# The last batch's second expert, run on 32 places in column tiles amid the main products

## The chip, the cores and the metric

One NeuronCore of a Trainium2 chip runs the whole program. The metric is the time of one execution on the device in microseconds; lower is better. Of each kernel there are several timed runs and one profiled execution, in which every instruction and DMA transfer is recorded. Engines: PE (TensorE, matrix products), DVE (VectorE), ACT (ScalarE), POOL (GpSimd), SP (SyncE, which here only issues DMA). Each engine takes its instructions strictly in order and waits on semaphores.

## The reference

Attention with 16 query heads and one key/value head, then a two-level mixture of experts on the result: a group is chosen per row, then an expert in the group.

```
scores = scale * q @ k^T ; attn = softmax(scores) ; out = attn @ v     # 8 batches, 16 heads, 384 rows, 64 wide
x = out, heads joined                                                  # 3072 rows x 1024
g_idx = argmax(x @ w_group)        ; g_w = softmax weight of the choice
e_idx = argmax(x @ w_expert[g])    ; e_w = softmax weight of the choice
y[row] = g_w * e_w * (relu(x[row] @ w1[g, e]) @ w2[g, e])              # 16 experts, 1024 x 1024 each
```

All inputs are random draws; rows of one batch are so alike that each of the batches 0 to 6 chooses one expert for all its 384 rows. Batch 7 chooses one expert for 363 rows and a second for 21.

## The kernel before, in words

**Order.** The order on every engine is written out by hand (`tc.manual_schedule`). A loop over 96 slots (line 794) does the attention: scores, softmax, transposes and the products with v, and, amid them, the expert of the batch before. An expert is a Python generator (`expert`, line 472) that yields after every four products and after each reading-out; `advance(n)` (line 710) takes 3n steps of it, so one `advance(1)` is one group of eight products with what reads it. An expert has eight groups of the first layer (L479, 128 x 384 in bfloat16, relu into `h_t`) and six of the second (L493, 128 x 512): three blocks j of 128 rows by two halves nh of the columns.

**Rows.** `main_expert` runs the most frequent expert of a batch on all 384 rows, each scaled by its gate weight (`gsel`), which is zero for a row that chose another. Each block of rows is stored by four DMAs of SP (L536, 32 rows of 4 KB each).

**The second expert of batch 7** has code of its own, `few_*`. `few_turn` turns xb back into rows (L587). `few_flags` and `few_places` give each row of the second expert a place by a running sum over the rows. With at most 128 such rows the expert is dealt with here, else it is left for the loop at the end. `few_places` makes a 0/1 matrix `sel` of 128 places per block. `few_gather` (L643) brings the rows to their places by products with `sel`, and (L654) the gate weight and the row's number in several bfloat16 parts. `few_expert` computes the hidden layer (L674: 64 products, 128 places) and the result (L689: 24 products), scales it (L693, L695), and one indirect DMA of POOL (L696) writes it over the 128 rows, places without a row being out of bounds. That DMA waits until the main stores have landed.

**The tail** (lines 827 to 908) is after slot 96: rest of batch 6's expert, last attention products, `load_second(0)` and `load_second(1)` (w1 and w2 of the second expert: POOL's DMAs with a cast from float32 to bfloat16, two halves each, L454; two buffers for w1 and two for w2, so the second expert's w2 waits for batch 6's last L493), then batch 7's main expert with the `few_*` steps between its groups, the gate arithmetic for the loop, `keep_xb` (L470, the last batch's xb to DRAM for the loop, 768 KB), `few_expert`. The loop at the end (L911) makes one pass for each (batch, expert) still open; here none.

**PSUM.** `xbank()` hands out four banks in turn (pool `ps_x`), `bank_end()` the four banks of the score tiles (`ps_s`, name `sb`) once attention has ended.

Of the kernel before, what the change touches and what calls it, by code (L numbers as in the profile page):

```python
# [19 lines left out]
def kernel(  # L20
# [24 lines left out]
    NR = 4096  # L45
    assert NR > N
# [9 lines left out]
    w2f = moe_w2.rearrange("g e (fo fi) d -> (g e) fi fo d", fi=P)  # L56

# [393 lines left out]
    def load_w(e, n):  # L451
        w = wpool.tile([P, KO, F], BF16, tag=f"w{n + 1}", name="w")
        for o in range(0, KO, 4):
            nc.gpsimd.dma_start(  # L454
                out=w[:, o:o + 4, :], in_=(w1f, w2f)[n][ds(e, 1), :, o:o + 4, :].rearrange("o p c f -> (o p) c f")
            )
        return w
# [72 lines left out]

    def main_expert(b, on_act):
        w1, w2 = st.pop(("w", b))

        def store(j, y):
            for n in range(QN):
                nc.sync.dma_start(out=out_v[b, j, n], in_=y[32 * n:32 * (n + 1), :])  # L536

        yield from expert(st["xb", b], w1, w2, scaled(lambda: st["gsel", b][0], store), any_bank, on_act)

    def few_ready():  # L540
# [4 lines left out]
        for name, t, widths in (  # L545
            ("16", c16, (("eye", P), ("tri", P), ("sel", ST * P), ("f", 4), ("cum", 4), ("parts", 5 * ST))),
            ("32", c32, (
                ("cols", P), ("tri", P), ("sel", ST * P), ("prod", ST * GE), ("ohs", GE), ("rows", ST), ("rest", ST), ("row", 1), ("pos", 4),
                ("f", ST), ("fits", 1), ("gate", 1), ("low", 1), ("at", 1),
# [7 lines left out]
            fw["cols32"], pattern=[[1, P]], base=0, channel_multiplier=0, allow_small_or_imprecise_dtypes=True  # L557
# [9 lines left out]

        rows, parts = fw["rows32"], fw["parts16"].rearrange("p (j t) -> p j t", t=5)
        nc.gpsimd.iota(
            rows, pattern=[[P, ST]], base=(B - 1) * S - NR, channel_multiplier=QN, allow_small_or_imprecise_dtypes=True  # L570
        )
        for n in range(QN):
            nc.gpsimd.memset(fw["low32"][32 * n:32 * (n + 1), :], float(n * (1 - 32 * QN)))
        nc.gpsimd.tensor_tensor(
            out=rows, in0=rows, in1=fw["low32"].to_broadcast([P, ST]), op=ALU.add
        )
        nc.gpsimd.tensor_copy(out=parts[:, :, 3], in_=rows)
        nc.gpsimd.tensor_tensor(out=parts[:, :, 4], in0=rows, in1=parts[:, :, 3], op=ALU.subtract)
        fw["xt"] = [ppool.tile([P, Dm], BF16, tag="pr", name="xtok") for _ in range(ST)]
        fw["xg"] = ppool.tile([P, KO, P], BF16, tag="pr", name="xg")  # L580
# [28 lines left out]
    def few_places():  # L609
# [6 lines left out]
        nc.vector.tensor_single_scalar(out=fw["fits32"], in_=pos[:, 3:4], scalar=float(P), op=ALU.is_le)  # L616
# [4 lines left out]
        for j in range(ST):  # L621
            nc.vector.tensor_scalar(
                out=fw["sel32"][:, ts(j, P)], in0=fw["cols32"], scalar1=pos[:, j:j + 1], scalar2=fw["f32"][:, j:j + 1],
                op0=ALU.is_equal, op1=ALU.mult,
            )
        nc.scalar.copy(out=fw["sel16"], in_=fw["sel32"])

    def few_parts():
        fw, gsel = st["few"], st["gsel", B - 1][1][:]
        parts, rest = fw["parts16"].rearrange("p (j t) -> p j t", t=5), fw["rest32"]  # L630
        nc.gpsimd.tensor_copy(out=parts[:, :, 0], in_=gsel)
        nc.gpsimd.tensor_tensor(out=rest, in0=gsel, in1=parts[:, :, 0], op=ALU.subtract)
        nc.gpsimd.tensor_copy(out=parts[:, :, 1], in_=rest)
        nc.gpsimd.tensor_tensor(out=parts[:, :, 2], in0=rest, in1=parts[:, :, 1], op=ALU.subtract)

    def few_gather():
        fw = st["few"]
        parts = fw["parts16"].rearrange("p (j t) -> p j t", t=5)
        for half in range(2):
            bank = xbank()  # L640
            for k in range(4):
                for j in range(ST):
                    nc.tensor.matmul(  # L643
                        out=bank[:, ts(k, P)], lhsT=fw["xt"][j][:, ts(4 * half + k, P)], rhs=fw["sel16"][:, ts(j, P)],
                        start=(j == 0), stop=(j == ST - 1),
                    )
            xg = fw["xg"][:, 4 * half:4 * half + 4, :].rearrange("p k t -> p (k t)")
            if half:
                nc.vector.tensor_copy(out=xg, in_=bank[:])
            else:  # L650
                nc.scalar.copy(out=xg, in_=bank[:])
        bank = xbank()
        for j in range(ST):
            nc.tensor.matmul(  # L654
                out=bank[:, 0:5], lhsT=fw["sel16"][:, ts(j, P)], rhs=parts[:, j, :], start=(j == 0), stop=(j == ST - 1)
            )
        nc.vector.tensor_reduce(out=fw["gate32"], in_=bank[:, 0:3], axis=AX.X, op=ALU.add)
        nc.vector.tensor_reduce(out=fw["row32"], in_=bank[:, 3:5], axis=AX.X, op=ALU.add)
        nc.vector.tensor_scalar(
            out=fw["at32"].bitcast(I32), in0=fw["row32"], scalar1=fw["fits32"], scalar2=float(NR), op0=ALU.mult,  # L660
            op1=ALU.add,
        )

    def few_expert():

        fw = st["few"]
        w1, w2 = st.pop("w_second")
        xg, gate, at_ = fw["xg"], fw["gate32"], fw["at32"].bitcast(I32)
        h_t = pool.tile([P, FO, S], BF16, tag="hT", name="few_h", bufs=1)
        for k0, k1 in ((0, 4), (4, 6), (6, FO)):  # L670
            bank = xbank()[:, 0:(k1 - k0) * P]
            for k in range(k0, k1):
                for ko in range(KO):
                    nc.tensor.matmul(  # L674
                        out=bank[:, ts(k - k0, P)], lhsT=w1[:, ko, ts(k, P)], rhs=xg[:, ko, :],
                        start=(ko == 0), stop=(ko == KO - 1),
                    )
            h, hp = h_t[:, k0:k1, 0:P], bank.rearrange("p (k t) -> p k t", t=P)
            if k0 == 4:
                nc.vector.tensor_scalar(out=h, in0=hp, scalar1=0.0, scalar2=None, op0=ALU.max)  # L680
            else:
                nc.scalar.activation(out=h, in_=hp, func=ACTF.Relu)
        cols = ((0, 512), (512, 768), (768, Dm))
        ys = [xbank()[:, 0:z - a] for a, z in cols]
        y = pool.tile([P, Dm], FP32, tag="y", name="few_y", bufs=3)
        for part in range(2):
            for (a, z), yp in zip(cols, ys):
                for fo in range(4 * part, 4 * part + 4):
                    nc.tensor.matmul(  # L689
                        out=yp, lhsT=h_t[:, fo, 0:P], rhs=w2[:, fo, a:z], start=(fo == 0), stop=(fo == FO - 1)  # L690
# [271 lines left out]
```

## Time and profile before

| what | us |
|---|---|
| timed runs, median of 3 (lowest, highest) | 509.68 (507.97, 509.74) |
| the profiled execution's own time | 508.39 |
| its span, first to last instruction | 507.0 |
| PE busy | 481.5 (95%) |
| DVE, ACT, POOL busy | 413.0, 321.8, 289.6 |

The span lies 1.39 us inside the profiled execution's time. In the profile, "L493" is line 493 of the kernel, `sb<-w,h_t` says that the tile sb is written from w and h_t, and a q behind an engine (SPq, POOLq) is its sequencer: waiting, branching or issuing a DMA. The chain of waits follows the work that ended last back from the last instruction: start, duration, what. A group row has: line, engine, operation, tiles, shapes, count, then busy us and mean ns of one, then the idle time before them and what ended it. In rows of DMA issues the last number is the time in us from issue to landing. Rows of DMA queues give packets, MB and the time their packets took as a share of 16 engines' time; q0 is the queue of POOL's DMAs, q1 that of SP's. A row of a stretch has its length, the busy time of PE, PEld, DVE, ACT and POOL with counts, the granted TensorE clock, DMA share and GB/s.

### The profile page before, as it was taken

What the parts mean: (1) busy time and instruction counts of PE and PEld (TensorE: products, weight loads), DVE (VectorE), ACT (ScalarE), POOL (GpSimd) and SP (SyncE); (2) the same over time, 40 slices, a digit from 0 to 9 for tenths busy, and PEclk for the clock granted to TensorE, in tenths of its full rate; (3) what the DMA queues carried; (4) which work ended last, traced back from release to release, by engine and by line L of the source; (5) the groups of instructions that cost most, each with busy time, mean ns of one, the idle gap of its engine ahead of it and who ended that gap; (6) DMA issues with size and microseconds to landing.
All of it is one profiled execution on the core that took longest, in us unless ns stands there. A gap on an engine that the chain in (4) does not pass through costs nothing.

```text
span 507.0 us, 20054 instructions
## 1 busy us (share of the span) xinstructions
PE 481.5 (95%) x8256; PEld 262.1 (52%) x8273; DVE 413.0 (81%) x737; ACT 321.8 (63%) x1002; POOL 289.6 (57%) x524
## 2 busy tenths in 40 slices
PE   7597789999999999999999999999999999999994
PEld 3143356555456455555465455555455455555653
DVE  3889979988899879988899879998799888890630
ACT  4776766677676766676676776676775775753421
POOL 1665955684576664584576654584476654584300
PEclk9999999999999999999999999999999999999998
DMA  7612997399947998389946998389956993089993
GB/s 106 145 26 45 174 239 193 76 160 233 255 86 129 220 237 218 75 157 232 261 84 123 217 243 223 75 143 230 245 116 111 210 241 110 1 155 241 231 243 121
DMA packets 64524, 84.04 MB, mean 166 GB/s; under 512 B 20379, under 2 KB 39963, under 8 KB 64432
## 3 DMA queue, kind: packets, MB, share of 16 engines
q0 software_dynamic: 19152, 37.84, 41.3%
q1 hardware_dynamic: 44320, 44.61, 35.2%
q8 instruction: 66, 1.08, 0.9%
q10 hardware_dynamic: 960, 0.30, 0.3%
q14 instruction: 26, 0.21, 0.1%
HBM read 101.52 MB, written 19.40 MB: 239 GB/s over the span
## 4 chain that ended last, share of the span: by engine, by line
PE 90%; DVE 5%; ACT 3%; issue 1%; POOL 0%; POOLq 0%; ACTq 0%; DVEq 0%
PE x L257 26%; PE s L206 25%; PE x L479 15%; PE x L493 13%; PE sb L493 4%; PE x L280 3%; ACT pr L220 3%; DVE nmx L217 2%; PE sb L479 2%; DVE ring L241 2%; PE x L674 1%; PE x L100 1%; PE x L689 1%; PE x L145 0%; PE x L643 0%
## 5 line engine op out<-in xcount | busy, mean ns | idle before, releaser
L235 POOL TENSOR_SCALAR pr<-pr,rinv 128x384 f32<-128x384 f32 x384 | 218.3, 588 | 146.0 <-DVE rinv L231 133.2
L220 ACT ACTIVATE pr<-s,nmx 128x384 f32<-128x384 f32 x384 | 218.0, 579 | 131.5 <-DVE nmx L217 120.0
L217 DVE TENSOR_REDUCE nmx<-s 128x2 f32<-128x768 f32 x192 | 174.3, 948 | 45.7 <-PE s L206 44.6
L241 DVE STREAM_TRANSPOSE ring<-pr 128x768 f32<-128x768 f32 x192 | 175.4, 952 | 0.1
L206 PE MATMUL s<-kt,qt 64*64 64x384 f32 x1536 | 148.9, 496 | 13.3 <-ACT pr L220 12.3
L257 PE MATMUL x<-ring,v_sb 32*64 32x256 f32 x4608 | 137.7, 378 | 0.2
L257 PEld LDWEIGHTS x<-ring,v_sb 32*64 32x64 f32 x4608 | 101.6, 131 | 43.0 <-issue 23.2
L206 PEld LDWEIGHTS s<-kt,qt 64*64 64x64 f32 x1536 | 48.5, 132 | 82.6 <-ACT pr L220 44.4
L220 ACT ACTIVATION_READ_ACCUMULATOR pr<-s,nmx 128x1 f32 x384 | 77.9, 203 | 0.0
L479 PE MATMUL x<-xb,w 128*128 128x384 bf16 x448 | 76.6, 326 | 0.0
L479 PEld LDWEIGHTS <-w 128*128 128x128 bf16 x512 | 47.7, 98 | 42.2 <-issue 12.6
L493 PE MATMUL x<-w,h_t 128*128 128x512 bf16 x276 | 64.7, 380 | 0.6
L493 PEld LDWEIGHTS <-h_t 128*128 128x128 bf16 x384 | 35.7, 98 | 52.0 <-issue 11.9
L454 POOL DMA_DIRECT2D w<-in_moe_w_dram x36 | 27.9, 784 | 10.8 <-issue 9.0
L271 ACT COPY xt<-x 128x256 f32<-128x256 f32 x96 | 28.9, 385 | 2.8 <-PE x L257 2.7
L485 ACT ACTIVATE h_t<-x 128x384 bf16<-128x384 f32 x56 | 25.4, 502 | 6.4 <-PE x L479 6.4
L272 POOL CAST xb<-xt 128x1024 bf16<-128x1024 f32 x24 | 24.9, 1036 | 3.6 <-ACT xt L271 3.6
L511 ACT ACTIVATE y<-x,gsel 128x512 f32<-128x512 f32 x36 | 24.8, 693 | 3.1 <-PE x L493 3.1
L195 DVE STREAM_TRANSPOSE qt<-q_sb 128x512 f32<-128x512 f32 x38 | 26.1, 687 | 0.0
L493 PE MATMUL sb<-w,h_t 128*128 128x512 bf16 x92 | 21.2, 379 | 0.2
L231 DVE RECIPROCAL rinv<-ssum 128x4 f32<-128x4 f32 x96 | 13.9, 144 | 3.3 <-ACT pr L220 3.3
L511 ACT ACTIVATE y<-sb,gsel 128x512 f32<-128x512 f32 x9 | 6.2, 688 | 16.1 <-PE sb L493 16.1
(132 smaller groups left out, 165.6 us busy)
## 6 DMA issues: line engine op xcount, KB each, us to landing
w<-in_moe_w_dram POOLq DMA_DIRECT2D x36, 1024.0 KB, 19.6
q_sb<-in_q_dram SPq DMA_DIRECT2D x76, 224.0 KB, 6.0
out_dram<-y SPq DMA_DIRECT2D x96, 128.0 KB, 6.3
xb_scratch<-xb SPq DMA_DIRECT2D x8, 768.0 KB, 4.3
v_sb<-in_v_dram SPq DMA_DIRECT2D x32, 96.0 KB, 4.0
kk<-in_k_dram SPq DMA_DIRECT2D x28, 92.0 KB, 4.1
q_sb<-in_q_dram SPq DMA_DIRECT2D x16, 128.0 KB, 3.3
q_sb<-in_q_dram SPq DMA_DIRECT2D x5, 64.0 KB, 3.1
```

Source lines behind the costliest of these rows:

```text
L195: nc.vector.transpose(out=qt[:].rearrange("p (x d) -> p x d", d=32), in_=q_sb[:, :, 0:32])
L206: nc.tensor.matmul(out=s[m * D:(m + 1) * D, h, 0:S], lhsT=qt[r, ts(2 * cc + m, D)], rhs=kt[r, :], start=True, stop=True, tile_position=(h ...
L217: nc.vector.tensor_reduce(out=nmx[:], in_=s[:, :, 0:S], axis=AX.X, op=ALU.max, negate=True)
L220: nc.scalar.activation(out=pr[:, h, :], in_=s[:, h, 0:S], func=ACTF.Exp, bias=nmx[:, h:h + 1], scale=1.0, accum_out=ssum[:, k, h:h + 1],)
L235: nc.gpsimd.tensor_scalar(out=pr, in0=pr, scalar1=rinv[:, k, h:h + 1], scalar2=1.0, op0=ALU.mult, op1=ALU.mult)
L241: nc.vector.transpose(out=ring[:, (u // 4) % 3, u % 4].rearrange("p h s -> p (h s)"), in_=st.pop(("pr", u))[:].rearrange("p h s -> p (h s)"),)
L257: nc.tensor.matmul(out=o[i][h * D:(h + 1) * D, 0:2 * P].rearrange("d (g c q) -> d g c q", g=2, c=4), lhsT=v_sb[r, n, :], rhs=ring[r, a:z + ...
L271: nc.scalar.copy(out=xt[:, :, ts(i, 32)], in_=o[:, 0:2 * P].rearrange("p (c q) -> p c q", c=KO))
L454: nc.gpsimd.dma_start(out=w[:, o:o + 4, :], in_=(w1f, w2f)[n][ds(e, 1), :, o:o + 4, :].rearrange("o p c f -> (o p) c f"))
L479: nc.tensor.matmul(out=hp[:, 0:S], lhsT=w1[:, ko, ts(fc, P)], rhs=xb[:, ko, :], start=(ko == 0), stop=(ko == KO - 1))
L493: nc.tensor.matmul(out=yp, lhsT=h_t[:, fo, ts(j, P)], rhs=w2[:, fo, ts(nh, 512)], start=(fo == 0), stop=(fo == FO - 1),)
L511: nc.scalar.activation(out=y[:, ts(nh, 512)], in_=yp, func=ACTF.Copy, scale=g)
```

## The change

The second expert has 32 places instead of 128 (with more rows it is left to the loop). With 32 places the rows are made the stationary side: `few_rows` runs, for each eighth o of the inner dimension, four products on four column tiles of 32, each with 256 of the 1024 columns of w, into one bank whose partition quarter c holds the columns of quarter c. `few_hidden` does the first layer so, transposes 32 x 32 blocks on DVE and takes the relu there; `few_out` does the second. For this, w2 of the second expert is loaded in another row order (`w2r`: partition fi holds rows 8 fi to 8 fi + 7, one contiguous run of 16 KB per half).

The result is not written by an indirect DMA. `few_put` transposes `sel`; `few_spread` brings the 32 rows to their places among the 128 rows of each block by a 0/1 product in float32 (four row tiles, one per quarter of the columns) and the scaled result is joined to the main rows in SBUF: added by DVE on y of the blocks 0 and 1, written by ACT first for block 2, to which DVE adds the main product. So the stores of each block come after its spread. `last_expert` replaces `main_expert` for batch 7: relu of every second group on DVE, block 2's stores by half rows, the last four of them in turn on SP and ACT. `few_hidden`, `few_out` and `few_spread` stand between the groups of the second layer. `keep_xb` is moved ahead of all stores of batch 7. The gate weights' and row numbers' parts (`few_parts`, lines 568 to 578, 652 to 662) go.

```
+    w2r = moe_w2.rearrange("g e (fi fo) d -> (g e) fi fo d", fi=P)
...
-        st.setdefault("w_second", []).append(load_w(st["e2"], n))
+        st.setdefault("w_second", []).append(load_w(st["e2"], n, (w1f, w2r)))
...
+    def store_rows(b, j, y, cols=slice(0, Dm), queues=(nc.sync,)):
+        for n in range(QN):
+            queues[n % len(queues)].dma_start(out=out_v[b, j, n][:, cols], in_=y[32 * n:32 * (n + 1), cols])
...
+    def last_expert():
+
+        w1, w2 = st.pop(("w", B - 1))
+        ys = st["ys"] = [pool.tile([P, Dm], FP32, tag="y", name="y", bufs=3) for _ in range(ST)]
+        banks = [bank_end] * FO + [lambda: xbank()[:]] * (2 * ST)
+
+        def result(j, nh, yp, by_act):
+            y, g = ys[j][:, ts(nh, 512)], st["gsel", B - 1][0][:, j:j + 1]
+            if j < ST - 1:
+                nc.scalar.activation(out=y, in_=yp, func=ACTF.Copy, scale=g)
+            else:
+                nc.vector.scalar_tensor_tensor(out=y, in0=yp, scalar=g, in1=y, op0=ALU.mult, op1=ALU.add)
+                store_rows(B - 1, j, ys[j], ts(nh, 512), (nc.sync, nc.scalar) if nh else (nc.sync,))
+
+        yield from expert(
+            st["xb", B - 1], w1, w2, result, lambda: banks.pop(0)(), lambda k: k % 2 == 0
+        )
...
     def few_gather():
         fw = st["few"]
+        bank = xbank()
+        for k in range(KO):
+            for j in range(ST):
+                nc.tensor.matmul(
+                    out=bank[:, ts(k, FEW)], lhsT=fw["xt"][j][:, ts(k, P)], rhs=fw["sel16"][:, j * P:j * P + FEW],
+                    start=(j == 0), stop=(j == ST - 1),
+                )
+        nc.scalar.copy(out=fw["xg"], in_=bank[:, 0:KO * FEW])
+
+    def few_put():
+
+        fw = st["few"]
         bank = xbank()
         for j in range(ST):
             nc.tensor.matmul(
+                out=bank[:, ts(j, P)], lhsT=fw["sel16"][:, ts(j, P)], rhs=fw["eye16"], start=True, stop=True
             )
+        nc.scalar.copy(out=fw["put32"], in_=bank[:, 0:ST * P])
+
+    def few_rows(lhs, w):
+
+        bank = xbank()
+        for o in range(KO):
+            for c in range(P // FEW):
+                nc.tensor.matmul(
+                    out=bank[ts(c, FEW), 0:256], lhsT=lhs[:, ts(o, FEW)], rhs=w[:, o, ts(c, 256)],
+                    start=(o == 0), stop=(o == KO - 1), tile_position=(0, c * FEW),
+                )
+        return bank[:, 0:256]
+
+    def few_hidden():
 
         fw = st["few"]
+        bank = few_rows(fw["xg"], st["w_second"][0])
+        nc.vector.transpose(
+            out=fw["h32"].rearrange("p (o t) -> p o t", t=FEW), in_=bank.rearrange("p (x o) -> p o x", o=FO)
+        )
+        nc.vector.tensor_scalar(out=fw["h16"], in0=fw["h32"], scalar1=0.0, scalar2=None, op0=ALU.max)
+
+    def few_out():
+        fw = st["few"]
+        bank = few_rows(fw["h16"], st.pop("w_second")[1])
+        nc.vector.tensor_copy(out=fw["y32"], in_=bank)
+
+    def few_spread(js):
...
+        for j in js:
+            a = 0 if j < 2 else 256
+            for c in range(P // FEW):
+                r = ts(c, FEW)
+                nc.tensor.matmul(
+                    out=parts[c // 2][:, c % 2, a:a + 256], lhsT=fw["put32"][r, ts(j, P)], rhs=fw["y32"][r, :],
+                    start=True, stop=True, tile_position=(c * FEW, 0),
+                )
+        for j in js:
+            a = 0 if j < 2 else 256
+            g, y = st["gsel", B - 1][1][:, j:j + 1], st["ys"][j]
+            for nh in range(2):
+                yv, part = y[:, ts(nh, 512)].rearrange("p (c d) -> p c d", c=2), parts[nh][:, :, a:a + 256]
+                if j == ST - 1:
+                    nc.scalar.activation(out=yv, in_=part, func=ACTF.Copy, scale=g)
+                else:
+                    nc.vector.scalar_tensor_tensor(out=yv, in0=part, scalar=g, in1=yv, op0=ALU.mult, op1=ALU.add)
+            if j < ST - 1:
+                store_rows(B - 1, j, y)
...
-    pending.append(main_expert(b, lambda k: k < FO or k % 2 == 0))
+    pending.append(last_expert())
...
     gate_count()
-    advance(1)
+    advance(2)
...
-    few_parts()
...
-    advance(3)
     few_gather()
+    advance(2)
+    few_put()
+    few_hidden()
     advance(2)
     ls_ps = xbank()
...
+    advance(1)
+    few_out()
+    keep_xb(b)
+    advance(1)
+    few_spread((0, 2))
+    advance(1)
+    few_spread((1,))
     advance(1000)
-    keep_xb(b)
-    few_expert()
```

In the built program, the body up to the last attention products stands as before on every engine. In the changed tail, in emission order: 8 L479, four `few_turn`, 8 L479, `few_flags`, two `few_turn`, 16 L479, `few_places`, 16 L479, the gate arithmetic, `few_gather`, 16 L479, `few_put`, `few_hidden`, block 0 (16 L493), half of block 1, `few_out`, `keep_xb`, the other half, `few_spread` of blocks 0 and 2, half of block 2, `few_spread` of block 1, the other half.

More of the change, by code (lines that the diff above doesn't have):

```diff
@@ L44 @@
     NP = B * GE
-    NR = 4096
-    assert NR > N
+    FEW = 32
     assert NP == P
@@ L666, in few_expert @@
+    def few_out():
         fw = st["few"]
[L667 to L682, printed above, removed]
```

85 lines of the change are left out of this document (17 added, 68 removed).

## The prediction

> **What bounds the kernel now.** I read the page first, then the chain of waits over the last 30 us, then single DMA issues with their landing times.
>
> ```profile
> PE 481.5 (95%) x8256; PEld 262.1 (52%) x8273; DVE 413.0 (81%) x737; ACT 321.8 (63%) x1002; POOL 289.6 (57%) x524
> PEclk9999999999999999999999999999999999999998
> PE 90%; DVE 5%; ACT 3%; issue 1%; POOL 0%; POOLq 0%; ACTq 0%; DVEq 0%
> ```
> ```profile
> 476.08 5.20 PE sb L479 x32
> 481.28 1.34 PE x L643 x24
> ...
> 486.20 6.91 PE sb L493 x32
> 493.11 3.57 PE x L674 x64
> 496.68 0.22 PE x L689
> ...
> 496.95 2.35 PE x L689 x14
> ...
> 499.38 0.76 DVE few_y L695
> ...
> 501.08 1.05 POOL out_dram L696
> ```
> TensorE carries 90% of the chain, and the body up to 476 us is not touched. In the tail the last batch's main products (L479, L493) run without a gap until 493.11. Only then comes the second expert: 3.57 us (L674), 2.6 us (L689), one scaling on DVE, one indirect store. All inputs of that stretch lie ready. So two things to ask: when are they ready, and what waits if PE comes for them earlier?
>
> ```profile
> 457.67 1.55 POOL L454 DMA_DIRECT2D w<-in_moe_w_dram  x2 [2.34 <-issue]
> 468.49 1.55 POOL L454 DMA_DIRECT2D w<-in_moe_w_dram  x2 [1.83 <-PE sb L493]
> w<-in_moe_w_dram POOLq DMA_DIRECT2D x1, 1024.0 KB, 24.8
> w<-in_moe_w_dram POOLq DMA_DIRECT2D x1, 1024.0 KB, 19.7
> w<-in_moe_w_dram POOLq DMA_DIRECT2D x1, 1024.0 KB, 25.4
> ```
> The second expert's w1 is issued at 457.67 and w2 at 468.49, in two halves each. The three landing times are, in order: second half of w1, first half of w2, second half of w2. With the second issue about 0.8 us behind the first, these halves land at 483.3, 488.2 and **494.7**. The last is 1.6 us after the main products end. Issuing w2 earlier is not possible: it waits for the previous main expert's last L493, which frees the buffer.
>
> **The change, part by part.**
>
> *PE work.* Removed after 493.11: 3.57 + 2.62 us up to DVE's release at 499.3, the DVE scaling, POOL's indirect store. Added amid the main products: `few_put` (3 products of 128 columns, 3 x 0.056 = 0.17 us from L674's 3.57/64), `few_hidden` and `few_out` (32 products of 256 columns each, on four column tiles), `few_spread` (8, then 4 float32 products on four row tiles). The gather keeps its 24 products, now 32 columns wide; I price it between a quarter and all of its old 1.34 us and take all. The tiles' concurrency comes from two rows:
>
> ```profile
> 468.19 1.03 PE x L280 x64
> 456.48 2.78 PE x L257 x96
> ```
> L280 runs 64 products of 64 columns on four column tiles, 1.03 us: 16 rounds of 64 columns at 1.0 ns a column in float32, so the tiles do overlap. In bfloat16 a column costs 0.44 ns (L674), so 8 rounds x 256 x 0.44 = 0.9 us for each of `few_hidden` and `few_out`; if they did not overlap, 3.6 us. L257 (eight tiles) gives 12 rounds x 256 columns in 2.78 us, 0.23 us a round: the spread is 0.46 + 0.23 us. Without any wait PE would end at 493.11 - 1.4 (gather and parts) + 1.34 + 0.17 + 0.9 + 0.9 + 0.7 = 495.7.
>
> *The waits that come in.* PE works in order. From 476.08 it has 16 products L479 (2.6 us), the gather (1.34), 16 more (2.6) and the put: it reaches `few_hidden` at 482.8 and its second half at 483.25. The second half of w1 landed at 483.3 before. Then 0.45, three L493 groups (8 x 6.91/32 = 1.73 each) and half of `few_out`: second half at 489.3 at the earliest, 5.4 us before w2's 494.7. This wait stands on PE with three L493 groups (5.2 us) and both spreads still behind it, and every store of the last batch behind those.
>
> When does w2 land now? Two edits move it.
> ```profile
> 487.06 8.83 SPq L536 DMA_DIRECT2D out_dram<-y  x12
> ```
> The stores of block 0 (rows 0 to 127), which began at 487 and shared the DMA engines with the rest of w2, now come after `few_out`. And `keep_xb` moves from SP's last place to right behind the previous batch's stores (about 471), so 768 KB go out while w1 and w2 are still coming in.
>
> ```profile
> q0 software_dynamic: 638, 1.27, 112.4%
> ```
> ```profile
> q0 software_dynamic: 484, 0.96, 85.0%
> q1 hardware_dynamic: 192, 0.52, 25.0%
> ```
> ```profile
> xb_scratch<-xb SPq DMA_DIRECT2D x1, 768.0 KB, 3.9
> ```
> The first row is 478 to 484: the weights alone move 0.212 MB a us, 4.95 us a half. So w2's second half, undisturbed, would land at 488.2 + 4.95 = 493.1. The next two are 471 to 477: beside 0.52 MB of stores the weights lost 0.31 MB, or 1.46 us, 2.8 us a MB. For 0.786 MB of xb that is 2.2 us. Bounds: nothing, and 3.9 us, its whole landing time. I take 2.2: w1's second half lands at 485.5, w2's at **495.3** (bounds 492.4 to 497).
>
> The new view of w2 makes each partition's half one run of 16 KB where there were four of 4 KB. No row shows such a load. The nearest rows are q0's own (638 packets of 4 KB read in 1.124 x 16 x 6 = 108 us of engine time, 23.5 bytes a ns) and the 6 KB runs of xb at the end:
>
> ```profile
> q1 hardware_dynamic: 145, 0.77, 95.9%
> ```
> That is 497 to 499: 0.77 MB in 30.7 us of engine time, 25.1 bytes a ns, 7% more. On two halves of 4.95 us it would save 0.7 us; I take nothing and keep 0.7 for the low bound. The Trainium skill, "DMA: Bandwidth & Descriptors", section Specifications, puts one DMA engine at about 27 GiB/s; w2's 0.212 MB a us is 0.424 MB read, 26.5 GB/s an engine, so by that page at most 9% is left, 0.8 us (an estimate), and the sum would be 512.0. The trace agrees that little is left.
>
> *From w2 to the end.* 495.3, rest of `few_out` 0.45, L493 1.73, spread of blocks 0 and 2 0.46: 497.95. Now a relay. In the built program ACT's copies of block 2 wait for DVE's additions to block 0, bank by bank, and the second half of the spread of block 1 waits for ACT's second copy.
>
> ```profile
> L407 DVE SCALAR_TENSOR_TENSOR end<-end,ohs_all 128x128 f32<-128x128 f32 x1 | 0.3, 291 | 0.0
> L511 ACT ACTIVATE y<-sb,gsel 128x512 f32<-128x512 f32 x8 | 5.5, 688 | 15.4 <-PE sb L493 15.4
> L513 DVE TENSOR_SCALAR y<-sb,gsel 128x512 f32<-128x512 f32 x3 | 2.3, 751 | 6.9 <-DMA out_dram<-y 2.7 <-PE x L894 2.5 <-PE sb L493 1.7
> ```
> DVE's multiply-add is priced between L513 (0.75) and four times L407 (1.16); I take 0.75, the same size. Two of them end at 499.45, ACT's second copy at 500.15, the spread at 500.4, the last L493 group at 502.1, the last multiply-add at 502.85.
>
> Then the stores. Before, blocks 0 and 1 left during the products. Now SP has 14 issues between 499.4 and the end, and two are ACT's. In the built program ACT's two hold the DMA semaphores that SP's third and fourth store of block 1 need, so these wait until ACT's two have **landed**, and SP's last two half rows come behind them.
>
> ```profile
> 461.84 1.72 SPq L536 DMA_DIRECT2D out_dram<-y  x4
> out_dram<-y SPq DMA_DIRECT2D x1, 128.0 KB, 2.1
> ```
> Four issues take 1.72 us, a store alone lands in 2.1. ACT issues at 502.9 and 503.3 and lands at 505.0 and 505.4; SP's four follow to 506.6, the last issued at 506.3, landing at 508.4. If the semaphores did not bind, SP's 14 issues alone would put the last at about 505.3 and save 1.0.
>
> Last, the end of the program: the indirect store was issued at 501.02 and landed 2.8 us later.
>
> ```profile
> 501.02 1.11 POOL L696 DMA_INDIRECT out_dram<-few_y,c  x1 [19.37 <-ACTq L911]
> out_dram<-few_y,c POOLq DMA_INDIRECT x1, 2.8
> ```
> From 503.8 to the span's end at 507.0 are 3.2 us; I take 3.0, as part of the final semaphores can pass beforehand. Span 508.4 + 3.0 = 511.4, 4.4 more. The profiled execution took 508.39 with a span of 507.0, so **512.8**. The three timed runs have a median of 509.68, 1.3 above the profiled one, so a timed median may come out by that much higher.
>
> Hidden, and why: `few_rows`' exact speed and the gather lie under the wait for w1 or w2 (if the column tiles did not overlap, only `few_out`'s second half would show, +1.3). Four of eight relus go from ACT to DVE, ahead of its gate arithmetic:
> ```profile
> 477.27 0.21 DVE L416 TENSOR_REDUCE es<-g_ex 128x15 f32<-128x60 f32 x1
> 482.00 0.35 DVE L887 TENSOR_SCALAR sel<-end,pcum,pw 128x128 bf16<-128x128 f32 x1
> ```
> That arithmetic takes 5.1 us; behind a relu that ends at 479.3 it ends at 484.4, the last relu at 485, and PE needs it at 487. POOL's dropped row numbers (L569 to L578) lie in slack.
>
> **Rivals.**
> - *The clock drops during the wait.* PE stands from 491.65 to 495.3, 3.65 us.
> ```profile
> 500.00:503.00 3.00, 0.15 (x2) 0.00 (x0) 0.13 (x1) 0.67 (x2) 1.11 (x1) 1.00 0.08 21
> 503.00:507.00 4.00, 0.00 (x0) 0.00 (x0) 0.00 (x0) 0.00 (x0) 0.00 (x0) 0.66 0.04 12
> ```
> The granted clock (third number from the end) is 1.00 up to 503 and 0.66 on average after that, with PE idle since 500.15: an idle stretch of about 3 to 4 us is enough, while the first page's line of slices shows 9 in every slice before. If it falls, the 6.3 us of PE work behind the wait slow down; between 0 and 6.3, I take 3: 515.8. The Trainium skill, "TensorE: Matmul & The Clock Gate", Part 1, says the clock halves after an idle window of about 3.4 us and that the window runs free; by that rule a 3.65 us wait holds a whole window only in some alignments.
> - *The weights come sooner.* Queues overlap better, xb costs nothing and the longer runs save their 0.7: w2 at 492.4, 509.9. For it: the DMA queues do not add up strictly. Against it: the 471 to 477 rows.
> - *No wait, faster.* The mechanism of the change works as drawn if w2's second half is there when PE is: by 489.3. Each us earlier than 495.3 is worth one; at 490.9 the change breaks even, at 489.3 it ends at 506.8, 1.6 faster. Against it: the load would have to gain 6 us on a queue that is full from its issue on.
> - *The change doesn't do what it says.* With over 32 rows the expert falls to the loop at the end, tens of us. A count on the reference's inputs gives 21 rows.
>
> **How the numbers follow.** Forecast 512.8, chance 0.57, its own range 511.0 to 514.5. Clock 0.13 (515.8), weights sooner 0.16 (509.9), no wait 0.06 (506.8), loop 0.02, the rest unforeseen, to either side. 0.5% (2.5 us) is about what a measurement of this kernel can tell from no change. Slower by more: 0.57 + 0.13 + 0.02 and 0.02 of the rest, 0.74. Within: weights sooner, no wait and a little of the rest, 0.23. Faster: 0.03. The range runs from the sooner weights to the dropped clock: 509.8 to 515.8.
>
> **What would show it.** Right: PE idle before L665 twice, released by DMA w; a landing of w2's second half near 495; about 14 SP stores after 499; two of them idle behind ACT's; span near 511. Wrong: w2 landing before 491, no PE gap over 1 us before `few_out`, or a granted clock below 1.00 around 495, where the relay and the stores would all be later than drawn.

## The result, and the profile after

| | before | after |
|---|---|---|
| median of the runs timed together, us (lowest, highest; 4 each) | 509.71 (507.97, 510.17) | 516.8 (514.75, 517.88) |
| ratio, 95% interval | | 1.0145 [1.0121, 1.0169] |
| the profiled execution's own time | 508.39 | 517.88 |
| its span | 507.0 | 516.0 |

The medians lie 7.1 us apart. The forecast of 512.8 was 4.4 us over the profiled execution of before and 3.1 over its median. Executions of one kernel spread by 2 to 3 us, those of before too (mean granted clock 0.988 to 0.998), and some show half clock for 3.4 or 6.8 us within the first 50 us (an early dip), which shifts all that follows. The page of after, its clock line and the shares of the chain that ended last:

```profile
PEclk9999999999999999999999999999999999999977
PE 78%; DVE 6%; DMA 5%; issue 4%; ACT 3%; POOL 2%; POOLq 0%; ACTq 0%; DVEq 0%
```

Before, the granted clock was full up to the last slice and no DMA stood in the chain's shares. Now two slices at the end are at 7 (the fall in the last one, at 510.86, lies behind TensorE's work), and DMA has 5%. The chain of waits of after, from w2's issue to the last result (start, duration, what):

```profile
469.19 25.44 DMA w<-in_moe_w_dram
...
494.68 1.04 PE x L665 x13
495.72 0.54 PE x L493
...
496.48 2.77 PE x L493 x6
499.25 1.76 PE part L695 x16
501.01 1.83 PE x L493 x8
502.84 1.16 PE part L695 x8
504.00 1.85 PE x L493 x8
...
505.88 0.75 DVE y L554
```

The chain enters TensorE with w2's second half (landed 494.63) and then goes through everything that was put behind `few_out`. Eight products of L493 take 1.83 us in the last groups, but right behind the wait eight (the record of one is missing) stretch over 3.53 us, from 495.72 to 499.25. The stretches of after say why (length, PE busy with count, granted clock, DMA share, GB/s; PE alone):

```profile
484.00:490.80 6.80, 5.76 (x40) 1.00 1.04 218
490.80:493.80 3.00, 0.70 (x17) 1.00 0.76 158
493.80:500.60 6.80, 5.71 (x35) 0.50 0.00 0
500.60:506.00 5.40, 5.24 (x32) 1.00 0.46 120
```

From 493.8 on TensorE runs at half speed for 6.8 us, the first of them while it still stands. Both waits, and what SP and ACT issue at the end, stand in the timeline of after:

```profile
484.99 0.62 PE L665 MATMUL x<-w,xg 128*32 128x256 bf16 x16 [2.28 <-DMA w<-in_moe_w_dram]
494.68 1.04 PE L665 MATMUL x<-w,xg 128*32 128x256 bf16 x16 [3.17 <-DMA w<-in_moe_w_dram]
502.56 9.42 SPq L533 DMA_DIRECT2D out_dram<-y  x14
506.71 2.13 ACTq L533 DMA_DIRECT2D out_dram<-y  x2
```

SP's 14 stores take 9.42 us, where four took 1.72 before; the last landed at 513.29, 7.4 us after the last multiply-add began.

### The profile page after: what moved, and what is told of

It is laid out like the page before. It is cut to its first block, busy times and chain, and to the rows that moved or that the text cites. A ratio compares the mean times of both kernels' runs of the same rounds, so it can differ in the third digit from the quotient of the medians.

```text
span 516.0 us, 20038 instructions
## 1 busy us (share of the span) xinstructions
PE 481.1 (93%) x8256; PEld 258.7 (50%) x8273; DVE 415.9 (81%) x741; ACT 319.9 (62%) x997; POOL 286.3 (55%) x511
## 3 DMA queue, kind: packets, MB, share of 16 engines
q8 instruction: 66, 1.08, 0.9%
## 4 chain that ended last, share of the span: by engine, by line
PE 78%; DVE 6%; DMA 5%; issue 4%; ACT 3%; POOL 2%; POOLq 0%; ACTq 0%; DVEq 0%
PE s L206 24%; PE x L257 23%; PE x L479 14%; PE x L493 14%; DMA w<-in_moe_w_dram 5%; DVE nmx L217 3%; ACT pr L220 3%; PE x L280 2%; DVE ring L241 2%; POOL pr L235 1%; PE part L695 1%; PE x L100 1%; POOL w L454 0%; PE x L145 0%; PE x L665 0%
## 5 line engine op out<-in xcount | busy, mean ns | idle before, releaser
L257 PE MATMUL x<-ring,v_sb 32*64 32x256 f32 x4608 | 137.2, 378 | 0.5 <-issue 0.4
L257 PEld LDWEIGHTS x<-ring,v_sb 32*64 32x64 f32 x4608 | 101.2, 131 | 43.2 <-issue 23.3
L493 PE MATMUL x<-w,h_t 128*128 128x512 bf16 x322 | 77.2, 385 | 0.9 <-issue 0.2
L479 PE MATMUL x<-xb,w 128*128 128x384 bf16 x448 | 76.6, 326 | 0.0
L479 PEld LDWEIGHTS <-w 128*128 128x128 bf16 x512 | 47.6, 98 | 42.1 <-issue 12.6
L493 PEld LDWEIGHTS <-h_t 128*128 128x128 bf16 x384 | 35.8, 99 | 53.5 <-issue 14.9
L280 PEld LDWEIGHTS x<-xt,wge 128*32 128x32 f32 x1024 | 12.7, 110 | 5.5 <-ACT y L511 2.5
L280 PE MATMUL x<-xt,wge 128*32 128x64 f32 (+1 forms) x1024 | 14.9, 210 | 0.0
```

Of the source, the lines that this page charges most:

```text
L257: nc.tensor.matmul(out=o[i][h * D:(h + 1) * D, 0:2 * P].rearrange("d (g c q) -> d g c q", g=2, c=4), lhsT=v_sb[r, n, :], rhs=ring[r, a:z + ...
L280: nc.tensor.matmul(out=lt_ps[ts(c, 32), 0:32 * (j1 - j0)].rearrange("e (j q) -> e j q", q=32), lhsT=wge[:, ko, :], rhs=xt[:, ko, :, ts(c, ...
L479: nc.tensor.matmul(out=hp[:, 0:S], lhsT=w1[:, ko, ts(fc, P)], rhs=xb[:, ko, :], start=(ko == 0), stop=(ko == KO - 1))
L493: nc.tensor.matmul(out=yp, lhsT=h_t[:, fo, ts(j, P)], rhs=w2[:, fo, ts(nh, 512)], start=(fo == 0), stop=(fo == FO - 1),)
```

## The experiments

My theory after this profile: TensorE's wait for w2, half clock behind it, and a float32 spread twice as long as drawn. Rivals: the transfers (xb ahead of w2) make the loss; or the stores at the end do, wherever TensorE stands. The kernel before was timed beside each batch (508.0 to 509.0), so ratios are what compares across batches.

**fill**: products on a blank tile fill the wait for w2.

```
     advance(1)
+    busy(12)
     few_out()
```

> The changed kernel with 12 products on a blank tile (0.216 us each, 2.6 us) put on PE ahead of few_out, inside the 3.2 us in which PE stands waiting for w2. Theory A (the wait lets the granted clock fall to half from 493.8 to 500.6 us, and few_out's second half, an L493 group and the first spread run at half speed): the clock stays at 1.00, the L493 group behind few_out takes 1.8 instead of 3.5 us, the last multiply-add on DVE starts 2.5 to 3 us earlier, the span falls from 516.0 to about 513. Theory B (the stores on SP set the end, whatever PE does): the clock stays up, but the span falls by less than 1 us. The blank products write a bank that nobody reads.

Profiled span 512.3, clock full to the end, last multiply-add begun at 502.83 instead of 505.88. Median 515.98, ratio 1.0146 [1.0129, 1.0163]: 3.7 us less span in the profiled executions (that of after is its slowest run), in the medians nothing. The first wait, 2.37 us here, was still open.

**noxb**: the last batch's rows are not kept for the loop, which has no pass here.

```
     few_out()
-    keep_xb(b)
```

> The changed kernel without the last batch's store of xb (768 KB to DRAM, which only a pass of the final loop would read; no pass is made). Tells what the moved store costs the weights. By the prediction's sum it delayed w2 by 2.2 us: w2's second half lands at about 492.5 instead of 494.6, PE waits about 1.1 instead of 3.2 us, the clock stays at 1.00, and the span falls by 2.1 + 2.5 to 3 us, to about 511. If the queues overlap and xb costs nothing: landing at 494.6, span 516.

w2's last landing 493.35, its transfer 1.7 us shorter than in after; TensorE, freed sooner by w1, still stands 3.17 us, and the clock halves behind it. Ratio 1.0138 [1.0114, 1.0162]. xb is not the loss.

**sponly**: all stores on SP.

```
-                store_rows(B - 1, j, ys[j], ts(nh, 512), (nc.sync, nc.scalar) if nh else (nc.sync,))
+                store_rows(B - 1, j, ys[j], ts(nh, 512), (nc.sync,))
```

> The changed kernel with all four of the last half-row stores on SP, none on ACT. Theory A (ACT's two stores hold the semaphores that SP's third and fourth store of block 1 wait for, and one issue on each queue takes 1.9 and 1.75 us while both issue): SP's 16 issues follow each other at 0.47 us, last issue at about 510, last landing about 511.8 instead of 513.3, the span falls by 1.5 us. Theory B (SP's number of issues is what counts): two issues more on SP, span 0 to 1 us longer.

From the last multiply-add's end to the last landing 6.04 us instead of 6.66; ratio 1.0133 [1.0092, 1.0175]. The semaphores that ACT's stores hold are real in the trace of after (SP's third store of block 1 went at 509.828, ACT's first landed at 509.81). Moving the stores is worth 0.6 us between these two traces, and nothing that the ratios can tell.

**later**: `few_out()` one L493 group later.

```
-    advance(1)
+    advance(2)
     few_out()
     keep_xb(b)
-    advance(1)
     few_spread((0, 2))
```

> The changed kernel with few_out one group of eight L493 products later, so that three such groups stand ahead of it instead of two and a half of the block pair: one group fewer behind the wait. Theory A: w2 lands at 494.6 as before, PE waits 1.4 instead of 3.2 us, the clock stays at 1.00; the last multiply-add starts 1.7 (the group) + 2.5 to 3 us (the clock) earlier, the span falls by about 4 us to 512. Theory B (the stores set the end): the stores still follow the spread one after the other, the span falls by less than 2 us.

The wait for w2 shrinks to 0.16 us, but the clock had already halved for 3.4 us in the first wait (2.50 us). Ratio 1.0115 [1.009, 1.014]: the lowest of these four, but all four intervals overlap.

**half_w2**: `few_out` takes the first half of w2 twice and leaves out the second (line ends cut short).

```
-    def few_rows(lhs, w):
+    def few_rows(lhs, w, held=KO):
...
-                    ... rhs=w[:, o, ts(c, 256)],
+                    ... rhs=w[:, o % held, ts(c, 256)],
...
-        bank = few_rows(fw["h16"], st.pop("w_second")[1])
+        bank = few_rows(fw["h16"], st.pop("w_second")[1], 4)
```

> few_out multiplies with the first half of w2 twice instead of both halves, so it no longer waits for w2's second half; this kernel does not compute the second expert's rows. Theory A (the loss is the wait for w2's second half, the lower clock behind that wait and a relay that is dearer than forecast): few_out runs at about 491 to 492, the last multiply-add of y starts near 500 (in the run with fillers it came 7.8 us after few_out), the last landing near 506.5, the span 509 to 510, the time 510.5 to 512.5. Theory B (the end is set by the stores of the joined rows on SP and ACT and by their landings, wherever TensorE stands): 514 to 516, with the last landing within 1.5 us of the changed kernel's.

Median 513.44, ratio 1.0087 [1.0055, 1.0118], 1 us above what I expected. No wait before `few_out`, and the last multiply-add begins 16.2 us after w1's landing instead of 20.9. But the wait for w1 (2.51 us) now halved the clock. The tail, from the start of the last multiply-add to the last landing, is 7.2 us (7.4 in after), so the stores follow TensorE and do not set the end by themselves: theory B falls.

**bothfill**: fill, and the wait for w1 filled too.

```
     few_put()
+    busy(10)
     few_hidden()
...
+    busy(12)
     few_out()
```

> Products on a blank tile fill both waits (10 ahead of few_hidden, 12 ahead of few_out), so TensorE never stands there. Theory A (the times of the changed kernel differ from run to run because the granted clock falls during one of the two waits): granted clock 0.994 or more in every run, times within 1 us of each other, median 513.5 to 514.5. Theory B (the clock falls for another reason, or the spread of times has nothing to do with it): clocks between 0.983 and 0.990 in some runs and times from 514 to 517 as before.

Clock 0.994 to 0.996 in all four runs, median 513.59, ratio 1.0102 [1.0065, 1.0138]. One run was at 515.16, so the spread was wider than I wrote. The stretches of bothfill, with the same columns:

```profile
490.00:493.80 3.80, 3.42 (x30) 1.00 0.64 134
493.80:500.60 6.80, 6.53 (x56) 1.00 0.11 23
```

The stretch that was at 0.50 in after is at 1.00. From w2's landing to the start of the last multiply-add bothfill and fill need 8.43 us each, after 11.25: **the clock costs 2.8 us** in the profiled execution; the medians give (1.0145 - 1.0102) x 509 = 2.2 us, with intervals that just overlap.

**unjoined**: no spread, nothing joined; main rows stored as they are ready, all on SP (the second expert's rows are dropped).

```
-                nc.vector.scalar_tensor_tensor(out=y, in0=yp, scalar=g, in1=y, op0=ALU.mult, op1=ALU.add)
-                store_rows(B - 1, j, ys[j], ts(nh, 512), (nc.sync, nc.scalar) if nh else (nc.sync,))
+                nc.vector.tensor_scalar(out=y, in0=yp, scalar1=g, scalar2=None, op0=ALU.mult)
+            if nh:
+                store_rows(B - 1, j, ys[j])
...
-    few_spread((0, 2))
-    advance(1)
-    few_spread((1,))
```

> Keeps few_hidden and few_out where they are, with their waits, but leaves out the spread, the joining and the stores that hang on them: the main rows are stored as they are ready, all on SP, and the second expert's rows are dropped. Theory A (joining costs several us at the end: two spread rounds among the last groups, the multiply-adds and the late stores of whole rows): last group of L493 ends 501 to 503, last landing 505 to 506.5, time 510 to 512, so that joining costs 5 to 6.5. Theory B (joining costs about what was forecast, 0.7 for the spreads and under 1 for the stores): 514.5 to 515.5.

Median 510.65, ratio 1.0037 [1.0018, 1.0056]. The chain of unjoined:

```profile
469.45 24.15 DMA w<-in_moe_w_dram
...
493.64 0.65 PE x L666 x16
494.29 0.54 PE x L493
...
495.05 6.15 PE x L493 x22
...
501.23 0.75 DVE y L554
```

The wait of 3.63 us and a short half clock are still there, yet the kernel is only 0.4% slower than before. Joining, with the stores that hang on it, costs up to 1.08% of 509, 5.5 us; the wait, its clock and xb the other 1.9 us. The split is rough: in unjoined xb is issued only at 490.25, behind block 0's stores (470.86 in after), so w1 lands 1.5 us and w2 1.0 us sooner, and the half clock lasts 3.4 us where after has 6.8.

**spread16**: y and `put` in bfloat16 (the second expert's rows are rounded before they are spread).

```
...
-                    out=parts[c // 2][:, c % 2, a:a + 256], lhsT=fw["put32"][r, ts(j, P)], rhs=fw["y32"][r, :],
+                    out=parts[c // 2][:, c % 2, a:a + 256], lhsT=fw["put16"][r, ts(j, P)], rhs=fw["y16"][r, :],
```

> The changed kernel with the second expert's rows rounded to bf16 ahead of the spread, so that the spread's products are bf16 instead of fp32 (the rounding changes the result a little). Theory A (an fp32 product is two passes, which is what made the spread 1.1 us where 0.46 was forecast): 8 and 4 records instead of 16 and 8, the first spread 0.5 to 0.6 us instead of 1.08, the second not under 0.6 since it waits for ACT to read the first one's bank; at full clock the last multiply-add starts 7.4 to 7.9 us after w2's last landing instead of 8.4. Theory B (the time of a spread goes into loading weights or waiting, not into passes): 1.0 us or more for the first, no change of the time.

The timeline of spread16:

```profile
496.02 0.62 PE L665 MATMUL x<-w,xg 128*32 128x256 bf16 x16 [3.19 <-DMA w<-in_moe_w_dram]
496.57 1.90 PE L493 MATMUL x<-w,h_t 128*128 128x512 bf16 x7
498.40 0.40 PE L695 MATMUL part<-rest,c 32*128 32x256 bf16 x8
498.73 1.90 PE L493 MATMUL x<-w,h_t 128*128 128x512 bf16 x8
500.57 0.28 PE L695 MATMUL part<-rest,c 32*128 32x256 bf16 x2
501.09 0.28 PE L695 MATMUL part<-rest,c 32*128 32x256 bf16 x2 [0.24 <-ACT y L705]
```

Eight records instead of sixteen for the same eight products, 0.40 us instead of 1.83 at half clock (1.15 in bothfill). The second spread stands 0.24 us behind ACT's copy, as the relay was drawn. From w2 to the last multiply-add 7.26 us: 1.17 less than 8.43. Ratio 1.0137 [1.0105, 1.0168]; the gain hardly shows, which led to the next.

And here a wait of 3.19 us left the clock full, where 3.17 in after did not. The traces settle why. Within each execution all changes of the granted clock lie a whole number of 3.413 us apart: in sponly it changes at 17.54, 24.37, 495.41, 498.82 and 509.06, which lie 2, 140, 141 and 144 times 3.413 us behind the first. Cut into such windows, the stretch around the wait for w2 is one window of after, then the two of spread16 (same columns, from TensorE's busy time on):

```profile
490.38:493.79 3.41, 1.12 (x19) 0.51 (x18) 0.00 (x0) 0.69 (x1) 0.00 (x0) 1.00 0.77 161
491.23:494.64 3.41, 1.60 (x21) 0.72 (x20) 0.39 (x3) 0.69 (x1) 0.00 (x0) 1.00 0.94 197
494.64:498.05 3.41, 1.98 (x22) 1.03 (x23) 0.42 (x1) 0.00 (x0) 0.00 (x0) 1.00 0.06 12
```

In after most of the wait falls into one window, TensorE is busy in it for 1.12 us, and half clock follows. In spread16 a boundary cuts the wait in two, TensorE is busy for 1.60 and 1.98 us, and the clock stays. The other traces fit: from 470 us on, half clock follows each window with up to 1.34 us of TensorE work (half_w2 1.30, oneissue 1.34) and one with 1.45 (later), full clock follows one with 1.44 (spread16's first wait) and each with 1.60 or more. In the first 50 us, where other products run, the border is less sharp: half clock followed windows with 1.49 to 1.77 us, full clock others with 1.62 and more.

**fill16**: the edits of bothfill and spread16 together.

> bothfill and spread16 in one kernel: blank products fill both of TensorE's waits, and the spread's products are bf16 (rounded). Theory A (the lower clock and the two passes of fp32 are separate terms): their gains add, 1.16 us less than bothfill from w2's landing to the last multiply-add (7.2 to 7.4 us) and a ratio to the kernel before of 1.007 to 1.009; what is then left over the kernel before, 3.5 to 4.5 us, is the wait for w2 ahead of the last groups and the later stores. Theory B (one stood in for the other): ratio 1.010 or more.

In the trace the two add, as theory A had it: 7.26 us at full clock. In the time this does not show: median 515.12, ratio 1.0115 [1.0085, 1.0145], where A had 1.007 to 1.009. The tail gave it back: from the start of the last multiply-add to the last landing 7.5 us, in bothfill 6.1. One store's issue on ACT took 1.89 us (504.47 to 506.35), and SP's last stores waited for ACT's landings. This kernel's profiled execution had an early dip as well (w2 landed at 495.99, in bothfill at 493.98).

**That stall** stands in all ten kernels that issue the last stores in pieces as after does (unjoined among them). In after SP's issue at 506.93 (1.91 us) and ACT's at 507.09 (1.75 us) both end at 508.84. The DMA queues of after in just these 2 us:

```profile
q1 hardware_dynamic: 67, 0.14, 32.5%
q10 hardware_dynamic: 45, 0.06, 15.1%
q8 instruction: 1, 0.02, 4.3%
q14 instruction: 1, 0.01, 1.7%
```

One packet of 16 KB on an instruction queue starts at 507.11, and it takes 1.36 us. In each of the ten kernels the long issue (1.4 to 2.0 us) began at most 0.2 us before such a packet. The bodies agree: in all sixteen traces every issue of SP or ACT of 1.4 us or more begins within 0.4 us of such a packet (before: 1.67 us at 369.03, packet at 369.17), while issues of up to 1.36 us also stand with none near (unjoined at 490.25). That is coincidence many times over, not proof: no run here takes the packet away, and why it stalls an issue stays open.

**scatter**: the other way round. The order and the indirect store of before, with the second expert on 32 places in column tiles; `few_out` scales y, which lies on 128 partitions (32 places by 4 column quarters), and stores it in 128 pieces. The last block's stores go on SP and ACT in turn. The cut is against the kernel before.

```
     advance(1000)
     keep_xb(b)
-    few_expert()
+    few_hidden()
+    few_out()
...
+            out=out.rearrange("n (c d) -> (n c) d", c=4),
```

> The order and the indirect store of the kernel before, with the second expert on 32 places in column tiles: all main groups and their stores first (last block's stores on SP and ACT in turn), then few_hidden and few_out, gate and row number taken on all 128 partitions, and one indirect store of 128 pieces of 1 KB. Theory A (column tiles save what they seem to, and only their place amid the main groups and the joining lost it): main groups end near 492.4, few_out 0.5 us after w2's landing at 494.6, indirect store issued at 497 to 498.5 (behind the landing of the main rows), landed near 501, time 505 to 507.5, so 2 to 4.5 under the kernel before. Theory B (the indirect store of four times as many pieces, or the wait for w2 with the clock behind it, takes the gain back): 508.5 to 510.5.

Median 506.89 (10 runs), ratio **0.9967 [0.9946, 0.9987]**: faster than before. TensorE waits for no weights (0.89 us for DVE's relu is all), the main rows landed at 497.20, the indirect store at 500.85. The sooner main rows alone can't be the gain: before, these had landed at 497.97, and the indirect store (501.02) followed the second expert's own rows, which were ready at 500.14.

**scatter2**: all three blocks of the last batch on both queues.

```
-                queue = nc.scalar if b == B - 1 and j == ST - 1 and n % 2 else nc.sync
+                queue = nc.scalar if b == B - 1 and n % 2 else nc.sync
```

> As scatter, with the stores of all three blocks of the last batch on SP and ACT in turn. In scatter the indirect store began at 498.37, 1.2 us behind the landing of the main rows' last piece (497.20), while its own data stood ready at 495.45. Theory A (the indirect store waits for the main rows, and these for SP's issues): last landing of the main rows 495.5 to 496.5, indirect store 1 us sooner, time 0.8 to 1.5 under scatter (0.995 of the kernel before). Theory B (the main rows' landings are held by the w2 transfer that runs until 493, not by the issues): within 0.5 us of scatter.

Median 505.94 (7 runs), ratio **0.9944 [0.9923, 0.9965]**, the fastest kernel here. The chain of scatter2:

```profile
486.73 8.02 DMA out_dram<-y
494.76 0.02 issue
494.78 2.86 DMA out_dram<-y
...
498.94 1.04 POOL out_dram L691
```

TensorE is no longer in it. A store of block 0 needs 8.02 us to land beside w2, the last store waits for its semaphore, and the indirect store waits for that. So the last landing (497.64) came no sooner than in scatter, against theory A. The intervals of scatter and scatter2 overlap.

**scatter1**: scatter with one store of 128 partitions for each block of the last batch.

```
-                queue.dma_start(out=out_v[b, j, n], in_=y[32 * n:32 * (n + 1), :])
+                nc.sync.dma_start(out=out_v[b, j], in_=y[:])
```

> As scatter, but each block of the last batch is stored by one instruction of 128 partitions instead of four of 32. Theory A (issues and the waits for semaphores that earlier stores hold set when the last piece lands): last landing near 495.5 and the indirect store 1 to 1.7 us sooner than in scatter. Theory B (four transfers move side by side and one moves alone, or bandwidth counts): the last landing at 497 or later, time that of scatter or up to 2 us more.

Median 516.11, ratio 1.0149 [1.012, 1.0178]: the last store alone takes 13.59 us, and the indirect store began at 507.95 instead of 498.37.

**oneissue**: the same in the changed kernel, for the last batch.

```
-            queues[n % len(queues)].dma_start(out=out_v[b, j, n][:, cols], in_=y[32 * n:32 * (n + 1), cols])
+            nc.sync.dma_start(out=out_v[b, j][:, :, cols], in_=y[:, cols])
```

> The changed kernel with one store of 128 partitions in place of four of 32 for all rows of the last batch (4 stores there instead of 16). Theory A (behind the last multiply-add the tail of 7.4 us from its start to the last landing is issues, waits for semaphores that earlier stores hold, and one issue that stalls): tail 4.5 to 5.5, time 2 to 3 under the changed kernel (ratio to before 1.009 to 1.011). Theory B (the tail is the transfers themselves): tail 6.5 to 7.5, ratio 1.013 to 1.016.

Median 527.34, ratio 1.038 [1.0347, 1.0413]: the largest miss. The DMA queues of oneissue from 510 to 522, when only these stores move:

```profile
DMA packets 407, 1.12 MB, mean 94 GB/s; under 512 B 13, under 2 KB 13, under 8 KB 406
q1 hardware_dynamic: 406, 1.12, 24.0%
```

Such stores keep a quarter of the 16 engines' time busy (24.0%) and move 94 GB/s. In scatter, from 493 to 497, when w2 has landed and stores of 32 partitions move with xb, the share is 0.99 and 325 GB/s. The issues are dear, but they are also what spreads the transfer.

**scatter_amid**: scatter2 with `few_hidden` ahead of the last main groups.

```
+    few_hidden()
     advance(1000)
     keep_xb(b)
-    few_hidden()
     few_out()
```

> scatter2 with few_hidden among the last main groups instead of behind them. Theory A (the indirect store waits for the landing of the main rows, so whatever stands ahead of the last main group delays the end): last main group and last landing about 1.0 to 1.2 us later than in scatter2, time 0.5 to 1.2 over scatter2 (ratio to before 0.995 to 0.997). Theory B (the second expert's own chain sets the end, and starting it sooner helps): time under scatter2's, ratio 0.992 to 0.994.

Median 508.64 (12 runs), ratio 0.9985 [0.9966, 1.0003]. The last main row landed at 500.20 instead of 497.64 (1.2 us of it are an early dip of the clock in this profiled execution, by which the product of L890 came later too), and the indirect store began at 501.43. Putting the second expert's first layer among the main groups costs 0.4% (2 us) where the wait for weights is only 0.16 us: theory A, at more than its price. The two ratios come from different batches, and their intervals lie next to each other.

## Why the prediction was wrong

The direction and the mechanism of the delay were right: TensorE stands before `few_out` for w2, and all that was put behind it moves with it. The step that failed is the one from w2's landing to the last multiply-add: 6.8 us forecast, 11.25 measured, with the clock put at nothing in the sum and the spreads at half their time. The span came out 4.6 us short (511.4 forecast, 516.0 profiled). By the prediction's own steps:

| step | forecast | after | difference |
|---|---|---|---|
| w2's second half lands | 495.3 | 494.63 | -0.7 |
| from there to the last multiply-add's start | 6.8 | 11.25 | +4.45 |
| of it at full clock (bothfill, fill) | 6.8 | 8.43 | +1.6 |
| of it the clock | 0 | 2.8 | +2.8 |
| from there to the last landing | 6.3 | 7.4 | +1.1 |
| to the span's end | 3.0 | 2.7 | -0.3 |

- **The clock** is the largest term, and it was in the text as a rival (chance 0.13, 515.8); a granted clock below 1.00 around 495 was also named as a sign of being wrong. Its price of 3 was right (2.8 in the profiled execution), its chance was not. I took the 3 to 4 us of idle time at the program's end as the least that is enough. The runs show half clock behind waits of 3.63 (unjoined), 3.20 (oneissue), 3.18 (sponly), 3.17 (after, noxb), 2.51 (half_w2) and 2.50 us (later), and full clock behind 3.19 and 2.59 (spread16), 2.76 (sponly's first wait), 2.37 (fill) and 2.28 (after's first). The Trainium skill, "TensorE: Matmul & The Clock Gate", Part 1, has an idle window of about 3.4 us that runs free, and I read it as needing a wait at least as long. The traces agree on the window's length and that it runs free; they differ in that it need not be idle: one with 1.45 us of TensorE work was enough (later). With the border at 1.5 us of work, the 3.65 us drawn escape only if a boundary cuts them almost in half, so by these windows the chance was about 0.9 (an estimate), not 0.13. There are two waits, so two chances each time; I had weighed only the longer.
- **How long it stays** follows the same windows. In after TensorE still stood for 0.9 us of the first half-clock window and was busy for 2.31 us of it (493.79 to 497.20): the half clock went on for a second one, 6.8 us in all. With 2.65 (sponly) and 3.20 us (noxb) it ended after one.
- **The spread** was priced from L257's row, 96 records read as 96 products. A float32 product leaves two records: L695 shows 16 for its eight products, and 8 once they are bfloat16. So L257's were 48 products, a round 0.46 us instead of 0.23, and the spreads 1.08 and 1.16 us instead of 0.46 and 0.23. This is most of the 1.6 (bfloat16 takes 1.17 away). L280's row has the same flaw, 32 products in its 64 records. What was read from it, that column tiles overlap, held: 32 products of `few_out` take 1.06 us (half_w2), where 0.9 was drawn and 3.6 without overlap. The relay behind the spreads ran as drawn: DVE, then ACT, then the second spread.
- **xb and w2.** xb costs the weights 1.7 us (2.2 forecast; noxb). The longer runs of w2 gained little: its second half came 4.84 us behind the first (after, noxb), 0.217 MB a us against 0.212; I had kept 0.7 us of it for the low bound. w2's landing was 0.7 sooner than drawn, inside its bounds.
- **The stores.** The order and the semaphores came as drawn, 14 issues of SP and two of ACT. The stalled issue of 1.9 us did not stand in the sum and accounts for the 1.1: in bothfill, where it fell ahead of the last multiply-add, this step took 6.1 us.
- **What I never asked** is whether the part that costs is the place or the joining. unjoined puts up to 5.5 of the 7.1 us on the joining and the stores behind it, scatter_amid puts about 2 us on the place of the first layer. The products on 32 places themselves are a gain: put after the main groups, with the indirect store and the last batch's stores on both queues, they make the kernel 0.6% faster.

## What to carry to other kernels

Work that waits for a late transfer belongs behind everything that does not need it: ahead of three ready groups and sixteen stores its wait was paid by all of them, and once more through the clock. In these traces' last batch, a wait that left TensorE at most 1.34 us of work in one window of 3.41 us was each time followed by at least one window at half speed, one that left it 1.60 us or more never. So a wait of 2 to 3.6 us is to be priced as wait plus a chance, which by the same count is high at the upper end (an estimate); blank products in both waits took the loss of clock away (bothfill). When a tile's price is read from a row, count its records against the products in the code first.

## What the hardware showed unexpectedly

- The clock can halve in a wait of 2.5 us and stay full through one of 3.19. It changes on boundaries 3.413 us apart, by TensorE's busy time in the window that ends; where the boundaries fall differs between executions.
- Stores of 128 partitions, rows in four interleaved groups, used a quarter of the DMA engines' time (24.0%, 94 GB/s), stores of 32 partitions, beside xb, almost all of it (0.99 in scatter). In oneissue this cost 2.3% over after.
- DMA issues on SP and ACT that mostly take 0.3 to 0.45 us took 1.4 to 2.0 us where a 16 KB instruction packet started beside them, in ten kernels out of ten; the cause is not shown.
